# Moving one value load behind a key load, and the last head's mixer steps and their sum to earlier pairs

## The chip, the cores and the metric

The kernel runs on one core of one Trainium2 chip. The metric is the device time of the whole program in microseconds (us), as the median of several runs. The profile used below is one further execution of the same program, recorded by the hardware profiler.

## What is computed

A decode step of attention over a large cache, with a token-mixing MLP beside it, both added to the input:

```python
B, Sq, D = 8, 1, 512
Hq, Hkv, Sk, Dh = 32, 8, 8192, 128          # 4 query heads per key/value head
xn = layernorm(x)
q  = (xn @ wq) as (B, Hq, 1, Dh)
scores = q . k_cache * Dh**-0.5              # k_cache, v_cache: (8, 8, 8192, 128) float32
o  = softmax(scores) . v_cache
A  = o @ wo
h  = layernorm(xn)                           # the mixer: F = 1792 hidden units over one token
u  = gelu(h[b, d] * w1[f] + b1[f])           # (B, D, F)
Bo = sum_f u * w2[f] + b2
out = x + A + Bo
```

Nearly all bytes are the two caches: 64 pairs (8 key/value heads by 8 batch rows), each with 4 MiB of keys and 4 MiB of values, some 537 MB; `wq` and `wo` add 8 MiB each.

## The kernel before

The unit of work is a pair (h, b), key/value head h and batch row b, both counted from 0. The pairs run in order, b fastest. Everything is float32. There are two buffers of 4 MiB for keys, `K[b % 2]`, and two for values, `V[b % 2]`; at the start the two value buffers hold the two halves of `wq` until the queries have been projected from them (L193).

All large loads are issued by SyncE (SP) into one queue. An issue waits until its buffer is free, and every later issue stands behind it. The order of instructions on every engine is the order of the code; no scheduler moves them.

The function `slot(h, b)` is the work around one pair:

- `q_place` writes the query weights `w` of the next pair (DVE, L214).
- `qk(b)` forms the scores `s` of this pair from turned keys (PE, L228, 16 matmuls, shown as 32 records). When it has ended, its key buffer is free, and SP issues the load of the keys two pairs on.
- `turn(b + 1, ...)` transposes the next pair's keys in place, in four quarters (DVE, L222, about 2.3 us each). The first one waits until these keys have landed.
- `sm_max` (DVE, L234), `sm_bias` (PE, L238, then DVE, L239 and L240) and `sm_exp` (ACT, L243) are the softmax; `sm_place` (PE, L247, and DVE, L248) lays the result out as `pt`.
- `pv(b - 1)` multiplies the pair before by its values (PE, L255, again 16 matmuls, into `o`). When it has ended, its value buffer is free, and SP issues the value load of pair b + 1.
- `o_pick` (DVE, L260 to L263) and `o_place` (PE, L266) collect the output of pair b - 1.
- For each head the mixer takes 14 steps. `mx_step(j)` is one gelu on ACT (L312), a product on POOL (L313) and, but for j = 0, an addition to `macc` on POOL (L315). Both work on one buffer `g`, so a step waits for the one before. `mx_end` (PE, L319) sums `macc` over its partitions after the last step, and `y_add(mixed)` (DVE, L297) adds this to the output.

Exp and gelu need different tables on ACT: each change from one to the other is an ACT_TABLE_LOAD in front of the instruction.

In heads 0 to 6 a pair takes two mixer steps, and the sum is formed in the next head's first pair. The last head has no next head, so its steps are closer: steps 0 and 1 in pair 1, and then three each in pairs 2 to 5 (steps 2 to 4, 5 to 7, 8 to 10, 11 to 13). Its `mx_end` stands behind `qk(6)`. The pairs 6 and 7 of the last head are written out by hand after the loops (L408 to L443). There the keys of pair 7 come in four pieces, its values in pieces of a half, a quarter and two eighths, and the last part of `wo`, called `wo_end`, is loaded into the key buffer that has become free. At the end stand `o_last` (L269 to L272), `o_scale` (L285), `o_project` (L293), `y_add(proj)` (L297) and the store of the output (L443).

At the start, SP's queue is: `wq` in two halves, keys of pair (0, 0) in four pieces, keys of (0, 1), values of (0, 0), values of (0, 1), then from the slots keys of (0, 2), keys of (0, 3), values of (0, 2) and so on.

Of the kernel before, what the change touches and what calls it, by code (L numbers as in the profile page):

```python
# [24 lines left out]
NF = F // P  # L25
# [7 lines left out]
def attn_mixer_kernel(ctx: ExitStack, tc: tile.TileContext, x, kc, vc, wq, wo, w1, b1, w2, b2, out):  # L33
# [22 lines left out]
    V = [ring.tile([P, NT, DH], F32, name=f"v{k}") for k in range(2)]  # L56
# [8 lines left out]
    def load(to, src, h, b, pieces=(NT,)):  # L65
        rows = src[b, h, :, :].rearrange("(p t) d -> p t d", p=P)
        at = 0
        for n in pieces:
            nc.sync.dma_start(to[b % 2][:, at:at + n, :], rows[:, at:at + n, :])
            at += n  # L70
# [4 lines left out]
    def load_wo(h):  # L75
        nc.sync.dma_start(wo_t, wo.rearrange("(h r p) n -> h p r n", p=P, r=REP)[h])
# [136 lines left out]
    def q_place(h, b):  # L213
        nc.vector.tensor_tensor(W[b % 2].rearrange("p j (x r) -> p j x r", r=REP),  # L214
                                QT[:, h, b].unsqueeze(2).to_broadcast([P, NB, 2 * NB, REP]),
                                imask.rearrange("p i k -> p (i k)").unsqueeze(1).unsqueeze(3).to_broadcast([P, NB, 2 * NB, REP]), ALU.mult)
# [3 lines left out]
    def turn(b, a, w=NT // 4):  # L220
        t = K[b % 2][:, a:a + w, :].rearrange("p t d -> p (t d)")
        nc.vector.transpose(t, t)  # L222

    def qk(b):
        kt = K[b % 2].rearrange("p (u g) d -> p g u d", g=NG)
        for j in range(NB):
            for g in range(NG):
                nc.tensor.matmul(S[b % 2][g * Q:(g + 1) * Q, :], W[b % 2][:, j, :], kt[:, g, :, j * Q:(j + 1) * Q],  # L228
                                 start=(j == 0), stop=(j == NB - 1))
# [3 lines left out]
    def sm_max(b):  # L233
        nc.vector.tensor_reduce(MR, S[b % 2], AX.X, ALU.max)  # L234

    def sm_bias():
        m = misc()
        nc.tensor.matmul(m[:, :P], MR.to_broadcast([P, P]), nident, start=True, stop=True)  # L238
        nc.vector.tensor_tensor(SQ, m[:, :P], hmask, ALU.add)  # L239
        nc.vector.tensor_reduce(NBIAS, SQ, AX.X, ALU.min)  # L240

    def sm_exp(b):
        nc.scalar.activation(PR[b % 2], S[b % 2], AF.Exp, bias=NBIAS, scale=SCALE, accum_out=LR[:, b:b + 1])  # L243

    def sm_place(b):
        m = misc()
        nc.tensor.matmul(m, perm, PR[b % 2], start=True, stop=True)  # L247
        nc.vector.transpose(PT[b % 2], m)  # L248
# [3 lines left out]
    def pv(b, u0=0, u1=NU):  # L252
        for u in range(u0, u1):
            c = u % NB
            nc.tensor.matmul(O[b % 2][c * Q:(c + 1) * Q, :], PT[b % 2][:, u * Q:(u + 1) * Q],  # L255
                             V[b % 2][:, u * NG:(u + 1) * NG, :].rearrange("p t d -> p (t d)"),
                             start=(u < NB), stop=(u >= NU - NB))

    def o_pick(b):
        nc.vector.tensor_tensor(OM.rearrange("p (g d) -> p g d", g=NG), O[b % 2].rearrange("p (g d) -> p g d", g=NG),  # L260
                                dm.unsqueeze(2).to_broadcast([P, NG, DH]), ALU.mult)
        nc.vector.tensor_add(OB, OM[:, :256], OM[:, 256:])  # L262
        nc.vector.tensor_add(OB[:, :DH], OB[:, :DH], OB[:, DH:])  # L263

    def o_place(b):
        nc.tensor.matmul(MH[:, b * REP:(b + 1) * REP], OB[:, :DH], sel, start=True, stop=True)  # L266
# [10 lines left out]
    def o_sums():  # L277
        for r in range(REP):
            nc.tensor.matmul(sums[:, r * B:(r + 1) * B], sel[:, r:r + 1].to_broadcast([P, P]), LR, start=True, stop=True)

    def o_recip():
        nc.vector.reciprocal(RD, sums.rearrange("p (r b) -> p r b", r=REP))

    def o_scale():
        nc.vector.tensor_tensor(OTS.rearrange("p r (b s) -> p r b s", s=BS)[:, :, :, 0],  # L285
                                MH[:, :REP * B].rearrange("p (b r) -> p r b", r=REP), RD, ALU.mult)
# [3 lines left out]
    def o_project(w):  # L290
        for r in range(REP):
            for j in range(NB):
                nc.tensor.matmul(proj[j * Q:(j + 1) * Q, :], OTS[:, r, :], w[:, r, quarter[j]],  # L293
                                 start=(r == 0), stop=(r == REP - 1))

    def y_add(m):
        nc.vector.tensor_add(yacc, m, yacc)  # L297
# [3 lines left out]
    def mx_pick(h):  # L301
        nc.vector.tensor_tensor(BM, ident[:B, bass.ds(h, 1)], ident[:B, bass.ds(h, 1)], ALU.mult)
        nc.vector.tensor_tensor(BW, bsel[:, h, :], bsel[:, h, :], ALU.mult)

    def mx_begin():
        nc.tensor.matmul(MI[2], BM.to_broadcast([B, P]), hn, start=True, stop=True)

    def mx_copy():
        nc.scalar.copy(HB, MI[2])

    def mx_step(j):
        nc.scalar.activation(G, HB, AF.Gelu_apprx_tanh, bias=b1t[:, j:j + 1], scale=w1t[:, j:j + 1])  # L312
        nc.gpsimd.tensor_tensor(G if j else ACC, G, w2t[:, j:j + 1].to_broadcast([P, D]), ALU.mult)  # L313
        if j:
            nc.gpsimd.tensor_add(ACC, ACC, G)  # L315

    def mx_end():
        for j in range(NB):
            nc.tensor.matmul(mixed[j * Q:(j + 1) * Q, :], BW, ACC[:, quarter[j]], start=True, stop=True)  # L319
# [18 lines left out]

    q_project(first_turns)
    load(V, vc, 0, 0)  # L340
    load(V, vc, 0, 1)
    q_place(0, 0)


# [1 line left out]
    def after(h, b, n):  # L346
        return (h, b + n) if b + n < B else (h + 1, b + n - B)

    def slot(h, b, last=False, first=False):

        q_place(*after(h, b, 1))
        qk(b)
        load(K, kc, *after(h, b, 2), (NT // 4,) * 4 if last and b == B - 3 else (NT,))
        if b == 0 and not first:
            o_sums()
            mx_end()
        if b == 1:
            if not first:
                o_project(wo_t)
            mx_begin()  # L360
        turn(b + 1, 0)
        sm_max(b)
        if b == 0 and not first:
            o_recip()
        turn(b + 1, quart)
        if b or not first:
            pv(b - 1)
            load(V, vc, *after(h, b, 1))
        turn(b + 1, 2 * quart)
        sm_bias()  # L370
        if b or not first:
            o_pick(b - 1)
            o_place((b - 1) % B)
        if b < 2 and not first:
            y_add(proj if b else mixed)
        if first and b:
            mx_copy()
            mx_step(0)
            mx_step(1)
        sm_exp(b)  # L380
        turn(b + 1, 3 * quart)
        sm_place(b)
        if b == 0:
            if not first:
                o_scale()
            mx_pick(h)
        if b == 1 and not first:
            mx_copy()
        for j in range(3 * b - 4, 3 * b - 1) if last else range(2 * b - 2, 2 * b) if b and not first else ():
            mx_step(j)  # L390
        if b == 3 and not last:
            load_wo(h)

    tc.prologue_barrier()
    slot(0, 0, first=True)
    slot(0, 1, first=True)
    with tc.For_i(0, HKV - 1, 1, iteration_sync="staggered", head_align_engines=[nc.tensor.engine]) as h:
        for b in range(2, B + 2):
            slot(*after(h, b, 0))
            if b % 2 == 0:  # L400
                for e in (nc.tensor, nc.vector, nc.scalar, nc.gpsimd):
                    tc.previous_stage_wait(e.engine)
            elif b < B + 1:
                tc.stage_boundary()
    h = HKV - 1
# [2 lines left out]
    L = B - 1  # L408
    q_place(h, L)
    qk(L - 1)  # L410
    mx_end()
    turn(L, 0)
    turn(L, quart)
    sm_max(L - 1)
# [57 lines left out]
```

## Time and profile before

| | us |
|---|---|
| median of 3 runs | 1301.13 (1301.08 to 1301.55) |
| the profiled execution, whole | 1302.48 |
| its span | 1298.7 |
| DVE busy | 809.2 (62%) |
| PE busy | 780.6 (60%) |
| ACT busy | 289.8 (22%) |
| POOL busy | 251.8 (19%) |
| main DMA queue | 99.1% of 16 engines' span, 553.67 MB |

The span is what the trace covers; the whole time has 3.78 us more around it. Several engines are busy for more than half of the span, but only the DMA queue is busy nearly throughout. An average over the span hides a short stretch at either end, so the rows of single stretches have to be read: windows of 2 us, the timeline of an engine, and the chain of work that ended last, which gives at each step what released it.

### The profile page before, as it was taken

Reading aid. Unit: us, or ns where it says so; the run is one execution under the profiler, and the core shown is the slowest. Engines: PE = TensorE matmul, PEld = TensorE weight load, DVE = VectorE, ACT = ScalarE, POOL = GpSimd, SP = SyncE. Lnnn points to the kernel's source line nnn. Section 1 sums busy time; section 2 is a strip of 40 time slices with the busy share of each in tenths; the row PEclk is TensorE's granted clock in tenths of the full one; section 3 lists DMA queues with packets and bytes.
Section 4 is the critical chain, followed back from the end, with each engine's and each line's share of the span. In section 5 each row is a group of like instructions: output and inputs, shape, how many; then the busy total and the mean of one; then the engine's idle time right before and its main releaser. Section 6 shows DMA issues by size and latency. Waiting matters only on the chain.

```text
span 1298.7 us, 13708 instructions
## 1 busy us (share of the span) xinstructions
PE 780.6 (60%) x5178; PEld 250.2 (19%) x5178; DVE 809.2 (62%) x860; ACT 289.8 (22%) x366; POOL 251.8 (19%) x226
## 2 busy tenths in 40 slices
PE   3646457546566556666476565575565664666657
PEld 2212112112122111211122111121111221121112
DVE  3566665665765756755656747656557656567673
ACT  0103211212202213113221222113132132122230
POOL 0012221122112122022121122212221121211430
PEclk9768688777787786787776786777877877777878
DMA  9989999999999999999999999999999999999996
GB/s 403 434 377 435 431 434 432 430 426 441 435 435 428 430 436 435 435 428 431 435 436 434 429 430 435 436 434 430 430 434 436 434 433 428 433 436 434 431 427 268
DMA packets 24451, 553.93 MB, mean 427 GB/s; under 512 B 2508, under 2 KB 2540, under 8 KB 6900
## 3 DMA queue, kind: packets, MB, share of 16 engines
q1 hardware_dynamic: 24292, 553.67, 99.1%
q8 instruction: 12, 0.20, 0.1%
q0 software_dynamic: 128, 0.02, 0.0%
q10 hardware_dynamic: 16, 0.02, 0.0%
q14 instruction: 3, 0.02, 0.0%
HBM read 553.69 MB, written 0.02 MB: 426 GB/s over the span
## 4 chain that ended last, share of the span: by engine, by line
DMA 52%; DVE 21%; PE 18%; ACT 4%; issue 1%; POOL 1%; SPq 0%; ACTq 0%; DVEq 0%
DMA k<-in_A_k_cache_dram 52%; DVE k L222 17%; PE s L228 12%; PE misc L247 4%; ACT L243 2%; ACT pr L243 1%; DVE mr L234 1%; PE o L255 1%; DVE nb L240 1%; DVE sq L239 0%; PE mh L266 0%; DVE om L260 0%; POOL macc L315 0%; POOL g L313 0%; DVE ob L262 0%
## 5 line engine op out<-in xcount | busy, mean ns | idle before, releaser
L222 DVE STREAM_TRANSPOSE k<-k 128x2048 f32<-128x2048 f32 x256 | 582.0, 2292 | 396.2 <-DMA k<-in_A_k_cache_dram 396.1
L228 PE MATMUL s<-k,w 128*32 128x512 f32 x2048 | 318.4, 774 | 11.5 <-DVE k L222 8.4
L313 POOL TENSOR_TENSOR g<-g,w2t 128x512 f32<-128x512 f32 x104 | 108.1, 1039 | 718.9 <-ACT g L312 703.1
L266 PE MATMUL mh<-sel,ob 128*128 128x4 f32 x126 | 36.4, 359 | 346.8 <-DVE ob L263 346.8
L255 PE MATMUL o<-v,pt 128*32 128x512 f32 x2048 | 234.8, 598 | 0.8 <-DVE pt L248 0.8
L243 ACT ACT_TABLE_LOAD x56 | 71.8, 1283 | 683.5 <-DVE nb L240 683.5
L247 PE MATMUL misc<-pr,perm 128*128 128x512 f32 x128 | 129.9, 1117 | 15.5 <-ACT pr L243 12.6
L315 POOL TENSOR_TENSOR macc<-macc,g 128x512 f32<-128x512 f32 x104 | 132.4, 1273 | 9.6
L228 PEld LDWEIGHTS s<-k,w 128*32 128x32 f32 x2048 | 73.2, 139 | 293.3 <-issue 235.9
L312 ACT ACTIVATE g<-hb,b1t,w1t 128x512 f32<-128x512 f32 x112 | 91.1, 813 | 136.4 <-POOL macc L315 126.5
L238 PE MATMUL misc<-nident,mr 128*128 128x128 f32 x128 | 34.0, 350 | 110.7 <-DVE mr L234 110.7
L266 PEld LDWEIGHTS mh<-sel,ob 128*128 128x128 f32 x126 | 30.8, 304 | 360.8 <-DVE ob L263 360.0
L255 PEld LDWEIGHTS o<-v,pt 128*32 128x32 f32 x2048 | 62.3, 111 | 155.4 <-issue 153.6
L243 ACT ACTIVATE pr<-s,nb 128x512 f32<-128x512 f32 x64 | 44.0, 687 | 130.3 <-DVE nb L240 129.7
L248 DVE STREAM_TRANSPOSE pt<-misc 128x512 f32<-128x512 f32 x64 | 45.2, 707 | 42.0 <-PE misc L247 42.0
L312 ACT ACT_TABLE_LOAD x54 | 69.3, 1283 | 1.4
L313 POOL TENSOR_TENSOR macc<-g,w2t 128x512 f32<-128x512 f32 x8 | 8.3, 1039 | 286.9 <-ACT g L312 286.9
L238 PEld LDWEIGHTS misc<-nident,mr 128*128 128x128 f32 x128 | 20.8, 204 | 166.6 <-DVE mr L234 160.4
L234 DVE TENSOR_REDUCE mr<-s 128x1 f32<-128x512 f32 x64 | 41.8, 653 | 4.8 <-PE s L228 4.8
L260 DVE TENSOR_TENSOR om<-o,dm 128x512 f32<-128x512 f32 x63 | 42.9, 681 | 0.3 <-issue 0.3
L247 PEld LDWEIGHTS misc<-pr,perm 128*128 128x128 f32 x128 | 31.8, 307 | 22.2 <-ACT pr L243 20.2
L214 DVE TENSOR_TENSOR w<-qt,imask 128x128 f32<-128x128 f32 x64 | 29.8, 466 | 0.2 <-DVE pt L248 0.2
(77 smaller groups left out, 204.6 us busy)
## 6 DMA issues: line engine op xcount, KB each, us to landing
v<-in_A_v_cache_dram SPq DMA_DIRECT2D x63, 4096.0 KB, 27.5
k<-in_A_k_cache_dram SPq DMA_DIRECT2D x62, 4096.0 KB, 21.3
v<-in_A_wq_dram SPq DMA_DIRECT2D x2, 4096.0 KB, 12.7
k<-in_A_k_cache_dram SPq DMA_DIRECT2D x8, 1024.0 KB, 24.5
wo<-in_A_wo_dram SPq DMA_DIRECT2D x7, 1024.0 KB, 29.5
v<-in_A_v_cache_dram SPq DMA_DIRECT2D x1, 2048.0 KB, 7.7
v<-in_A_v_cache_dram SPq DMA_DIRECT2D x1, 1024.0 KB, 9.3
v<-in_A_v_cache_dram SPq DMA_DIRECT2D x2, 512.0 KB, 10.1
```

The costliest lines, as they stand in the source:

```text
L222: nc.vector.transpose(t, t)
L228: nc.tensor.matmul(S[b % 2][g * Q:(g + 1) * Q, :], W[b % 2][:, j, :], kt[:, g, :, j * Q:(j + 1) * Q], start=(j == 0), stop=(j == NB - 1))
L234: nc.vector.tensor_reduce(MR, S[b % 2], AX.X, ALU.max)
L238: nc.tensor.matmul(m[:, :P], MR.to_broadcast([P, P]), nident, start=True, stop=True)
L243: nc.scalar.activation(PR[b % 2], S[b % 2], AF.Exp, bias=NBIAS, scale=SCALE, accum_out=LR[:, b:b + 1])
L247: nc.tensor.matmul(m, perm, PR[b % 2], start=True, stop=True)
L248: nc.vector.transpose(PT[b % 2], m)
L255: nc.tensor.matmul(O[b % 2][c * Q:(c + 1) * Q, :], PT[b % 2][:, u * Q:(u + 1) * Q], V[b % 2][:, u * NG:(u + 1) * NG, :].rearrange("p t d - ...
L266: nc.tensor.matmul(MH[:, b * REP:(b + 1) * REP], OB[:, :DH], sel, start=True, stop=True)
L312: nc.scalar.activation(G, HB, AF.Gelu_apprx_tanh, bias=b1t[:, j:j + 1], scale=w1t[:, j:j + 1])
L313: nc.gpsimd.tensor_tensor(G if j else ACC, G, w2t[:, j:j + 1].to_broadcast([P, D]), ALU.mult)
L315: nc.gpsimd.tensor_add(ACC, ACC, G)
```

## The change

Two edits, which do not touch each other.

The load of the second values, pair (0, 1), no longer stands ahead of the slots. It is issued in slot (0, 0), by the same line that issues the value load in all other slots, and so behind the keys of pair (0, 2).

In the last head, the 12 mixer steps from 2 to 13 stand four each in pairs 2, 3 and 4, and none in pair 5. `mx_end` moves from behind `qk(6)` to the end of pair 5's slot, and so ahead of `qk(6)`.

```diff
     q_project(first_turns)
     load(V, vc, 0, 0)
-    load(V, vc, 0, 1)
     q_place(0, 0)
...
         if b or not first:
             pv(b - 1)
-            load(V, vc, *after(h, b, 1))
+        load(V, vc, *after(h, b, 1))
...
-        for j in range(3 * b - 4, 3 * b - 1) if last else range(2 * b - 2, 2 * b) if b and not first else ():
+        for j in range(4 * b - 6, min(4 * b - 2, NF)) if last else range(2 * b - 2, 2 * b) if b and not first else ():
             mx_step(j)
...
+        if b == 5 and last:
+            mx_end()
...
     qk(L - 1)
-    mx_end()
     turn(L, 0)
```

On SP, at the start of the program, with `v_86` and `v_87` the two value buffers and `k_84` and `k_85` the two key buffers. Before:

```order
L69 DMA k_84<-in_A_k_cache_dram 128x2048 x4
L69 DMA k_85<-in_A_k_cache_dram 128x8192
L69 DMA v_86<-in_A_v_cache_dram 128x8192
L69 DMA v_87<-in_A_v_cache_dram 128x8192
L69 DMA k_84<-in_A_k_cache_dram 128x8192
L69 DMA k_85<-in_A_k_cache_dram 128x8192
```

And now:

```order
L69 DMA k_84<-in_A_k_cache_dram 128x2048 x4
L69 DMA k_85<-in_A_k_cache_dram 128x8192
L69 DMA v_86<-in_A_v_cache_dram 128x8192
L69 DMA k_84<-in_A_k_cache_dram 128x8192
L69 DMA v_87<-in_A_v_cache_dram 128x8192
L69 DMA k_85<-in_A_k_cache_dram 128x8192
```

The keys of pair (0, 2), into `k_84`, have changed places with the values of pair (0, 1), into `v_87`; all that comes after them is as it was.

On PE, in the last head: the end of pair 5's slot (`o_place`, `sm_place`), then `qk(6)` (L228), `sm_bias(6)` (L238) and `pv(5)` (L255), as one piece of the difference:

```order
 L266 MATMUL mh<-sel,ob 128x4
 L247 MATMUL misc_174<-pr_157,perm 128x512
+L319 MATMUL mh<-macc,bw 32x128 x4
 L228 MATMUL s_169<-k_84,w_152 32x512 x16
-L319 MATMUL mh<-macc,bw 32x128 x4
 L238 MATMUL misc_175<-nident,mr 128x128
 L255 MATMUL o_172<-v_87,pt_155 32x512 x16
```

The four matmuls of the mixer's sum have moved from behind `qk(6)` to in front of it.

On ACT, in the last head, from the gelus of pair 4 to the exps of pairs 5 (`pr_157`), 6 (`pr_156`) and 7 (`pr_157`), as one piece of the difference:

```order
 L312 ACT_TABLE_LOAD
-L312 ACTIVATE g<-hb,b1t,w1t 128x512 x3
+L312 ACTIVATE g<-hb,b1t,w1t 128x512 x4
 L243 ACT_TABLE_LOAD
 L243 ACTIVATE pr_157,lr<-s_170,nb 128x512
-L312 ACT_TABLE_LOAD
-L312 ACTIVATE g<-hb,b1t,w1t 128x512 x3
-L243 ACT_TABLE_LOAD
 L243 ACTIVATE pr_156,lr<-s_169,nb 128x512
 L243 ACTIVATE pr_157,lr<-s_170,nb 128x512
```

Pair 4 has one gelu more, as pairs 2 and 3 have; pair 5's three gelus are gone, and with them the table load ahead of them and the one ahead of pair 6's exp.

## The prediction

> **What bounds the kernel now.** I read the page first: its line of GB/s, and the shares of the chain that ended last.
>
> ```profile
> GB/s 403 434 377 435 431 434 432 430 426 441 435 435 428 430 436 435 435 428 431 435 436 434 429 430 435 436 434 430 430 434 436 434 433 428 433 436 434 431 427 268
> DMA 52%; DVE 21%; PE 18%; ACT 4%; issue 1%; POOL 1%; SPq 0%; ACTq 0%; DVEq 0%
> ```
>
> Each of the 40 slices is 32.5 us. From the fourth to the last but one they hold 426 to 441 GB/s, so the queue carries all that it can there, and work between can be moved about without effect. Three slices fall short: the first, the third (377) and the last. The change touches the last two of these places. I then cut the third slice finer, by windows (us, busy time of each engine, granted clock of PE, DMA share, GB/s):
>
> ```profile
> 88.00:90.00 2.00, 2.00 (x12) 0.39 (x8) 0.61 (x1) 0.00 (x0) 0.00 (x0) 0.50 0.70 295
> 90.00:92.00 2.00, 2.00 (x20) 0.56 (x16) 0.07 (x1) 0.00 (x0) 0.00 (x0) 0.90 0.15 66
> 64.00:120.00 56.00, 31.58 (x194) 9.53 (x190) 36.85 (x36) 13.99 (x18) 10.44 (x10) 0.76 0.95 406
> 200.00:1200.00 1000.00, 610.06 (x3911) 190.29 (x3904) 636.35 (x652) 226.17 (x284) 193.08 (x168) 0.76 1.00 433
> ```
>
> The queue runs dry at 90 us. Against 433 GB/s, the 56 us at 406 have lost 56 x (1 - 406/433) = 3.5 us. What was late is in SP's own timeline (start, us, line, operation):
>
> ```profile
> 35.27 0.81 SPq L69 DMA_DIRECT2D v<-in_A_v_cache_dram  x2
> 43.45 18.34 SPq L69 DMA_DIRECT2D k<-in_A_k_cache_dram  x2
> 66.07 0.33 SPq L69 DMA_DIRECT2D v<-in_A_v_cache_dram  x1
> 92.10 0.35 SPq L69 DMA_DIRECT2D k<-in_A_k_cache_dram  x1
> ```
>
> In the chain, a DMA's length runs from issue to landing:
>
> ```profile
> 43.45 29.42 DMA k<-in_A_k_cache_dram
> 92.10 12.17 DMA k<-in_A_k_cache_dram
> 120.95 26.57 DMA k<-in_A_k_cache_dram
> 164.83 21.33 DMA k<-in_A_k_cache_dram
> 242.90 20.68 DMA k<-in_A_k_cache_dram
> 280.81 24.17 DMA k<-in_A_k_cache_dram
> ```
>
> And on DVE the first turn of keys (0,1), which had waited for them:
>
> ```profile
> 43.91 2.31 DVE L222 STREAM_TRANSPOSE k<-k 128x2048 f32<-128x2048 f32 x1 [4.02 <-DMA k<-in_A_k_cache_dram]
> ```
>
> The two value loads, pairs (0,0) and (0,1), are issued together at 35.27. Keys (0,1) land at 43.91. Keys (0,2), issued at 43.45, land at 43.45 + 29.42 = 72.87, three loads later (values 0, values 1, keys 2): 28.96/3 = 9.65 us a load. In the loop, landings at 120.95 + 26.57 = 147.52 and 164.83 + 21.33 = 186.16 lie four loads apart: 38.64/4 = 9.66. Where a load of `wo` lies between (263.58 to 304.98) the step is 41.40, so 1 MiB of `wo` takes 2.75. On this grid keys (0,3) end at 82.5 and values (0,2), issued at 66.07, at 92.2. Keys (0,4) are issued at 92.10: nothing is queued ahead of them. They wait for `qk(2)`, which waits for keys (0,2), which stood behind values (0,1), which nobody needed yet.
>
> Now the tail, by the timeline (start, us, engine and line; in brackets the idle time before and its releaser):
>
> ```profile
> 1259.23 4.57 PE L228 MATMUL s<-k,w 128*32 128x512 f32 x32
> 1264.91 0.65 DVE L234 TENSOR_REDUCE mr<-s 128x1 f32<-128x512 f32 x1
> 1267.13 1.26 POOL L315 TENSOR_TENSOR macc<-macc,g 128x512 f32<-128x512 f32 x1
> 1268.44 0.65 PE L319 MATMUL mh<-macc,bw 128*32 128x128 f32 x8 [4.64 <-POOL macc L315]
> 1269.03 0.80 PE L238 MATMUL misc<-nident,mr 128*128 128x128 f32 x2
> 1269.75 6.13 PE L255 MATMUL o<-v,pt 128*32 128x512 f32 x32
> 1270.62 1.28 ACT L243 ACT_TABLE_LOAD   x1 [4.69 <-DVE nb L240]
> 1270.66 4.50 DVE L222 STREAM_TRANSPOSE k<-k 128x2048 f32<-128x2048 f32 x2
> 1276.87 3.64 PE L228 MATMUL s<-k,w 128*32 128x512 f32 x32
> 1281.74 3.64 PE L255 MATMUL o<-v,pt 128*32 128x512 f32 x32
> 1290.31 1.92 PE L255 MATMUL o<-v,pt 128*32 128x512 f32 x16
> 1294.15 1.08 PE L293 MATMUL mh<-k,ots 128*32 128x128 f32 x32 [0.31 <-DVE ots L285]
> ```
>
> And two windows of it (PE's clock is the last but two):
>
> ```profile
> 1266.00:1268.00 2.00, 0.00 (x0) 0.00 (x0) 0.00 (x0) 0.00 (x0) 1.91 (x2) 1.00 1.14 492
> 1270.00:1272.00 2.00, 2.00 (x12) 0.40 (x8) 1.90 (x4) 1.37 (x2) 0.00 (x0) 0.50 1.06 459
> ```
>
> PE has ended `qk(6)` at 1263.80 and then stands 4.64 us in front of the mixer's sum, whose last POOL step ends at 1268.39. Behind it in PE's order waits `sm_bias(6)`, whose input is there at 1265.5; behind that on DVE the last two turns, and `qk(7)` at 1276.87 behind these and behind `pv(5)`. The idle time also costs clock: 1.00 before, 0.50 after, so `pv(5)` takes 6.13 where `pv(6)` takes 3.64. From `qk(7)` on PE hardly waits until the projection at 1294.15. So the tail is bound by PE and its wait for POOL, not by the queue.
>
> **The change part by part.** *The load.* Its issue (under 0.4 us on SP) moves past one issue, keys (0,2), which waits until 43.45 for `qk(0)`. Behind `qk(0)` the queue still holds values (0,0), to 43.91 + 9.66 = 53.6, so nothing runs dry; POOL's queue is not passed. Keys (0,2) then land at 63.2 and values (0,1) at 72.9, before `pv(1)` in the next slot wants them (keys (0,3) at 82.5 come first). All of slot 1 behind its first turn comes 9.66 earlier, keys (0,4) are issued near 82.4 with 10 us still queued, and the dry stretch is gone. Its price has three readings. Keys (0,4) landed at 104.27 where the grid has 72.87 + 3 x 9.66 = 101.85: 2.4. The bytes say 3.5. And keys (0,6) landed at 147.52, seven loads and one `wo` behind 72.87, where the grid has 72.87 + 67.6 + 2.75 = 143.2: 4.3. The first is taken when 16 engines start together on an empty queue and none lags, the last between two landings with a full queue. I take the bytes, which lie between: **3.5**, with 2.4 and 4.3 as ends. Since the queue is the bound up to the tail, all of it should arrive there.
>
> *The steps.* A fourth step is added to pairs 2, 3 and 4:
>
> ```profile
> 1226.41 0.81 ACT L312 ACTIVATE g<-hb,b1t,w1t 128x512 f32<-128x512 f32 x1 [2.51 <-POOL macc L315]
> 1235.70 1.28 ACT L243 ACT_TABLE_LOAD   x1 [8.48 <-DVE nb L240]
> 1247.72 1.28 POOL L315 TENSOR_TENSOR macc<-macc,g 128x512 f32<-128x512 f32 x1
> ```
>
> A step takes 0.81 + 2.50 = 3.31 us. The third gelu of pair 3 ends at 1227.22, a fourth at 1230.5, and the next exp's table load starts at 1235.70: 5 us of cover, so 0. In pair 4 the last addition now ends at 1249.00 + 3.31 = 1252.3. If this cover went, each further us would delay exp, `sm_place` and the next `qk`, though in pairs 2 to 4 still before the queue's bound.
>
> *The sum.* It reaches PE at 1259.2, 6.9 us after that addition, waits for nothing, and takes 0.65. It delays `qk(6)` to 1264.45, while `sm_max(6)` stands behind two turns until 1264.91: hidden, by 0.46. Without that cover its excess would be paid in full.
>
> *What then comes earlier.* `sm_bias(6)` starts at 1265.5 instead of 1269.03, that is 3.53 earlier, and takes 0.49 to 0.80. DVE's last turns end at 1270.66 + 4.50 - 3.53 = 1271.6. PE idles only 1.1 us; it had none to do from 1263.80 to 1268.44, and the window up to 1268 still shows 1.00, so the clock should hold, and `pv(5)` runs from 1266.1 to 1269.7. Exp(6) needs no table load (its 1.28 is gone, but lies beside `pv(5)`), and `sm_place(6)` ends at about 1270.9. `qk(7)` waits for the turns: 1271.6 instead of 1276.87, **5.3** earlier. Behind it the same instructions follow at the same clock, if the queue keeps up:
>
> ```profile
> 1249.07 27.68 SPq L69 DMA_DIRECT2D v<-in_A_v_cache_dram  x5
> 1276.84 0.96 SPq L81 DMA_DIRECT2D k<-in_A_wo_dram  x2
> ```
>
> The same transfers by size, with the us from issue to landing:
>
> ```profile
> v<-in_A_v_cache_dram SPq DMA_DIRECT2D x1, 4096.0 KB, 27.2
> v<-in_A_v_cache_dram SPq DMA_DIRECT2D x2, 512.0 KB, 10.1
> k<-in_A_wo_dram SPq DMA_DIRECT2D x1, 256.0 KB, 12.1
> ```
>
> Values 6 land at 1249.07 + 27.2 = 1276.3; `pv(6)` wants them at 1281.74 - 5.3 = 1276.4. Values 7 are now issued from about 1268 to 1270, well before the queue is empty, so by the grid they end at 1286.0 (`pv(7)`'s last part wants them at about 1286.5), and `wo_end` at 1288.7 (`o_project` wants it at 1294.15 - 5.3 = 1288.85). These fit with 0.1 to 0.5 to spare. If the last landing came no earlier than now, at the second issue of `wo`, about 1277.3, plus 12.1 = 1289.4, 4.75 would be left. So the tail gives 4.75 to 5.3; I take **5.2**, since its loads no longer wait for `pv(5)`.
>
> The sum: 3.5 + 5.2 = 8.7 off a span of 1298.7, so 1290.0, and 1293.8 for the profiled execution with its 3.78 around. That execution took 1302.48, 1.35 more than the median of the runs, so the median should go from 1301.13 to **1292.4**.
>
> **The rivals.** *The head gives little.* If the lag from 104.27 to 147.52 is not owed to the dry queue, the head gives 2.0 to 2.4, and the time is 1301.1 - 2.2 - 5.2 = 1293.7. For it: the landing at 104.27 is a direct measurement; against it: the bytes. Here the Trainium skill bears on the head: "DMA: Bandwidth & Descriptors", section "Anatomy of one DMA", gives each DMA a fixed cost of about 2.0 us, which a queue that never empties hides (it states this for another kind of queue than SP's). By it the head would give 2.0, an estimate from that page, and the time would be 1293.9; the row of 12.17 against 9.66 has 2.5.
>
> *The tail's clock stays at half.* If the clock drops in spite of the shorter gap, `pv(5)` takes 6.13 and `sm_place(6)` 2 us, so `qk(7)` starts at 1274.3: the tail gives 2.6 and the time is 1295.0. For it: `pv(5)` ran so now. Against it: the clock held for over 4 us of idle PE. The Trainium skill's "TensorE: Matmul & The Clock Gate", part on the HAM clock gate, has the clock fall after an idle window of about 3.4 us; a gap of 1.1 us is below that too.
>
> *The load changes nothing.* Were the third slice's loss due to something else, only the tail's 5.2 would stay: 1295.9. The issue at 92.10 with the queue empty speaks against it.
>
> *Slower: the sum stalls PE ahead of `qk(6)`.* Now only the softmax of pair 6 waits behind the sum; then `qk(6)` and all behind it would. It decides once the four steps of pair 4 end later than 1259.2, at 3.31 + 6.9/4 = 5.0 us a step. To end 0.2% (2.6 us) above now it must also eat the 8.7: 18.2 us over four steps, 7.9 us a step, for 1305 or so. The gelu at 1226.41 had waited 2.51 for POOL while DVE and PE were busy beside it, so a step of 7.9 us is remote.
>
> **How the numbers follow.** 0.2%, 2.6 us, is about what a measurement of this kernel can tell from no change. Forecast 0.62; little from the head 0.2; half clock in the tail 0.08; no gain from the load 0.04; less than 2.6 us either way, by several of these, 0.03; slower 0.03. The likeliest lies between 3.5 + 5.2 = 8.7 and its ends: 4.3 + 5.3 = 9.6 (1291.5) and 2.4 + 4.75 = 7.15 (1294.0). The range goes on to the half-clock case, 1295.0, and a little below the ends, since I have no row for the queue's last microseconds at full rate: 1290.8 to 1295.2. It leaves out some 0.12 (the last three cases, and a little of the first). Faster 0.94, same 0.03, slower 0.03.
>
> **What would show it.** Right: no window near 90 us below 250 GB/s, a third slice of 430 or more, keys (0,2) landing near 63, keys (0,4) issued near 82 and landing 20 us later; on PE, the sum without a wait in front of it, `pv(5)` near 3.6 us, some 5 us less from `qk(6)`'s end to `qk(7)`'s start. Wrong: a new dip later in the first 150 us, PE waiting for value pieces or `wo_end` by more than 1 us near the end, or a clock of 0.50 during `pv(5)`.

## The result, and the profile after

The changed kernel takes 1294.2 us (median of 5 runs, 1293.86 to 1294.46) where the kernel before, in the same series, takes 1301.55 (1301.08 to 1301.82): 7.35 us less, a ratio of 0.9944 with a 95% interval of 0.993 to 0.9959. The forecast was 1292.4 with a range of 1290.8 to 1295.2. Its profiled execution took 1293.86, where the forecast had 1293.8 for it, with a span of 1290.5.

The page's line of GB/s no longer has a dip in its third slice, and the queue's share has gone from 99.1% to 99.7%:

```profile
GB/s 405 428 433 430 431 436 436 428 436 431 432 437 431 433 435 429 436 436 428 437 431 433 437 427 436 435 430 436 432 431 437 432 432 435 429 436 434 429 427 331
q1 hardware_dynamic: 24292, 553.67, 99.7%
```

The windows of the head (busy times, PE's clock, DMA share, GB/s) now carry 430 GB/s over the 56 us that had 406, and the nearly empty window at 90 us (66 GB/s before) is gone:

```profile
88.00:90.00 2.00, 0.00 (x0) 0.00 (x0) 1.90 (x3) 0.00 (x0) 0.00 (x0) 0.93 0.87 377
90.00:92.00 2.00, 0.39 (x2) 0.39 (x2) 1.87 (x5) 1.80 (x2) 0.00 (x0) 0.50 0.99 426
64.00:120.00 56.00, 33.95 (x206) 9.91 (x202) 36.21 (x36) 13.41 (x17) 12.63 (x11) 0.76 1.00 430
```

The chain of waits, where a DMA's length runs from issue to landing, shows why: keys (0,2) land at 43.09 + 19.82 = 62.91, and keys (0,4) are issued at 81.68 instead of 92.10, with some 20 us from issue to landing instead of 12.17. The third row is keys (0,6), which land at 143.40 instead of 147.52:

```profile
43.09 19.82 DMA k<-in_A_k_cache_dram
81.68 19.88 DMA k<-in_A_k_cache_dram
119.47 23.93 DMA k<-in_A_k_cache_dram
```

In the tail, PE's timeline has the sum (L319) without a wait, `sm_bias(6)` at 1261.88, `pv(5)` at full clock (3.64 instead of 6.13) and `qk(7)` at 1267.75. New is the bracket of `pv(6)`, in the fifth row: it waits for a DMA.

```profile
1255.84 0.65 PE L319 MATMUL mh<-macc,bw 128*32 128x128 f32 x8
1261.88 0.49 PE L238 MATMUL misc<-nident,mr 128*128 128x128 f32 x2 [1.59 <-DVE mr L234]
1262.30 3.64 PE L255 MATMUL o<-v,pt 128*32 128x512 f32 x32
1267.75 3.64 PE L228 MATMUL s<-k,w 128*32 128x512 f32 x32 [0.76 <-DVE k L222]
1273.35 3.64 PE L255 MATMUL o<-v,pt 128*32 128x512 f32 x32 [0.66 <-DMA v<-in_A_v_cache_dram]
1281.92 2.11 PE L255 MATMUL o<-v,pt 128*32 128x512 f32 x16
1285.92 1.08 PE L293 MATMUL mh<-k,ots 128*32 128x128 f32 x32 [0.31 <-DVE ots L285]
```

### The profile page after: what moved, and what is told of

It reads as the page before. It is cut to its first block, busy times and chain, and to the rows that moved or that the text cites. A ratio compares the mean times of both kernels' runs of the same rounds, so it can differ in the third digit from the quotient of the medians.

```text
span 1290.5 us, 13705 instructions
## 1 busy us (share of the span) xinstructions
PE 778.6 (60%) x5178; PEld 249.8 (19%) x5178; DVE 809.2 (63%) x860; ACT 287.5 (22%) x364; POOL 252.1 (20%) x226
## 3 DMA queue, kind: packets, MB, share of 16 engines
q1 hardware_dynamic: 24292, 553.67, 99.7%
## 4 chain that ended last, share of the span: by engine, by line
DMA 53%; DVE 20%; PE 18%; ACT 3%; issue 2%; SPq 0%; DVEq 0%; ACTq 0%
DMA k<-in_A_k_cache_dram 51%; DVE k L222 16%; PE s L228 12%; PE misc L247 4%; DMA v<-in_A_v_cache_dram 2%; ACT L243 2%; ACT pr L243 1%; DVE mr L234 1%; PE o L255 1%; DVE nb L240 1%; DVE sq L239 0%; PE mh L266 0%; DVE om L260 0%; DVE ob L262 0%; DVE yacc L297 0%
## 5 line engine op out<-in xcount | busy, mean ns | idle before, releaser
L228 PE MATMUL s<-k,w 128*32 128x512 f32 x2048 | 319.0, 776 | 11.3 <-DVE k L222 9.2
L255 PE MATMUL o<-v,pt 128*32 128x512 f32 x2048 | 232.4, 593 | 1.5 <-DVE pt L248 0.8
L228 PEld LDWEIGHTS s<-k,w 128*32 128x32 f32 x2048 | 73.4, 139 | 292.4 <-issue 235.0
L238 PE MATMUL misc<-nident,mr 128*128 128x128 f32 x128 | 32.7, 339 | 101.8 <-DVE mr L234 101.6
L255 PEld LDWEIGHTS o<-v,pt 128*32 128x32 f32 x2048 | 62.1, 110 | 154.2 <-issue 151.5
L248 DVE STREAM_TRANSPOSE pt<-misc 128x512 f32<-128x512 f32 x64 | 45.3, 707 | 41.6 <-PE misc L247 41.6
L238 PEld LDWEIGHTS misc<-nident,mr 128*128 128x128 f32 x128 | 20.0, 196 | 158.5 <-DVE mr L234 155.1
```

## Experiments

Two quantities are read from every trace. The *head's shift* is how much earlier the keys of pair (0,6) land than at 147.52 in the first trace. The *tail's length* is the time from the first turn of the keys of pair (7,6), which waits for their landing, to the projection (L293): 1247.16 to 1294.15 = 47.0 us before, 1243.77 to 1285.92 = 42.15 after. Since the queue is full between the two, a gain in the one should add to a gain in the other.

**The load alone.**

```diff
-    load(V, vc, 0, 1)
...
-            load(V, vc, *after(h, b, 1))
+        load(V, vc, *after(h, b, 1))
```

> Only the load is moved; steps and sum as in the kernel before. Additive theory: keys (0,4) are issued near 82 and the dry stretch at 90 us goes; every key landing from pair (0,6) on comes 3.6 to 4.1 us earlier, and that shift is kept to the end, so about 1297.7. Rival, no part of the last head's loss of 0.8 us belongs to the steps: then this kernel also loses 0.8 us of its shift at the keys of pair (7,4), as the changed kernel did, and ends near 1298.3.

1297.73 us (9 runs, 1297.56 to 1299.24) against 1301.16 of the kernel before (15 runs, 1299.94 to 1302.70): 3.4 us less, ratio 0.9973 (0.9963 to 0.9983). The keys of pair (0,6) come 4.35 us earlier. The tail's length is 1244.08 to 1291.07 = 47.0, as before. So the load acts on the head only, and by the medians its price is close to what was forecast. The shift is not kept to the end, though: it falls from 4.4 to 3.1 us over the last head's pairs 3 to 6, without any change to the steps. Of the two theories put down, the first one's time came out, 1297.7, but the second one's loss of 0.8 us or more was there in the trace. The profiled run, 1299.24, is one of the two slowest of the nine, 1.5 us above the median, so the record does not say whether the seven faster runs lost it too.

**The tail alone.**

```diff
-        for j in range(3 * b - 4, 3 * b - 1) if last else range(2 * b - 2, 2 * b) if b and not first else ():
+        for j in range(4 * b - 6, min(4 * b - 2, NF)) if last else range(2 * b - 2, 2 * b) if b and not first else ():
...
+        if b == 5 and last:
+            mx_end()
...
-    mx_end()
```

> Only the steps and the sum are moved; the load as in the kernel before. Additive theory: no shift up to the last head, the sum without a wait, qk(7) 5.7 us earlier, and 4.1 to 4.9 us less at the projection: 1296.6 to 1297.4. If the fourth step in pair 2 is what costs the 0.8 us at the keys of pair (7,4), they land 0.8 us later than in the kernel before. Rival, the tail gains only because the queue is ahead from the start: less than 3 us.

1297.36 us (6 runs, 1296.07 to 1298.24) against the same 1301.16: 3.8 less, ratio 0.9968 (0.9956 to 0.998). The tail's length is 1246.66 to 1288.96 = 42.3, so 4.7 less. There is no loss at the keys of pair (7,4): the shift against the first trace is 0.5 us from pair (0,6) to the end. So the fourth step in pairs 2 to 4 costs nothing that this trace shows, and the loss comes only with the other edit. The two parts, 3.4 and 3.8, make 7.2 of the 7.35: they add, as far as intervals of more than 1 us to either side can tell.

**The steps alone, the sum in its old place.** The first two lines of that diff, without the others.

> Only the steps are closer, four each in pairs 2 to 4; the sum stays behind qk(6), the load as before. Theory: the wait for POOL goes because the steps have ended, so the sum runs at once in its old place, and the time is that of steps and sum together within 0.4 us. Rival, the place of the sum carries the gain: no more than 1 us faster than before.

1296.77 us (5 runs, 1296.44 to 1297.31), 4.4 less, ratio 0.9966 (0.9952 to 0.9979). PE's timeline has the sum behind `qk(6)` with no wait, and `sm_bias(6)` waiting for DVE as in the changed kernel:

```profile
1258.06 4.31 PE L228 MATMUL s<-k,w 128*32 128x512 f32 x32
1262.20 0.39 PE L319 MATMUL mh<-macc,bw 128*32 128x128 f32 x8
1264.10 0.49 PE L238 MATMUL misc<-nident,mr 128*128 128x128 f32 x2 [1.52 <-DVE mr L234]
```

The tail's length is 1245.99 to 1288.00 = 42.0. The medians of this and of steps and sum together are 0.6 apart, a little over the 0.4 expected, with intervals that overlap; the tails' lengths differ by 0.3. The steps carry the gain, and moving the sum adds nothing that shows.

**The sum alone, steps as before.** The last two pieces of that diff, without the first two lines: the forecast's slower rival.

> Only the sum is moved ahead of qk(6); three steps a pair up to pair 5, the load as before. This is the forecast's slower rival made to happen. Theory: PE stands in front of qk(6) from 1259.2 to 1268.4, qk(6) starts near 1269 at half clock, sm_bias(6) near 1274.2, the last turns end near 1280.4, and qk(7) starts 3.5 us later than before: about 1305. Rival, the place of the sum does not matter: within 0.5 us of before.

1305.91 us (6 runs, 1305.60 to 1306.75), 4.75 more than before, ratio 1.0037 (1.0024 to 1.0049).

```profile
1267.23 0.65 PE L319 MATMUL mh<-macc,bw 128*32 128x128 f32 x8 [9.13 <-POOL macc L315]
1267.65 6.18 PE L228 MATMUL s<-k,w 128*32 128x512 f32 x32
1274.66 0.49 PE L238 MATMUL misc<-nident,mr 128*128 128x128 f32 x2 [0.82 <-DVE mr L234]
1280.53 3.64 PE L228 MATMUL s<-k,w 128*32 128x512 f32 x32 [0.75 <-DVE k L222]
```

PE stands 9.13 us in front of the sum, and `qk(6)` behind it then runs at the low clock (0.50 in the windows from 1266 to 1272), 6.18 us instead of 4.57 before. The tail's length is 1245.96 to 1297.81 = 51.85, 4.9 more than before; I had expected 3.5. The mechanism is as described, and the same edit that is harmless behind four steps a pair costs nearly 5 us behind three.

**Half of values 6 left out.** On the changed kernel:

```diff
-        load(V, vc, *after(h, b, 1))
+        load(V, vc, *after(h, b, 1), (NT // 2,) if last and b == B - 3 else (NT,))
```

> The changed kernel, but the values of the last head's pair 6 are only half loaded (2 MiB left out; the other half of the buffer keeps old values). All later loads come 4.8 us earlier. Theory: the new tail is bound by the queue by less than 1 us, and right behind that by PE's own order from qk(7) on, so only PE's wait for values 6 (0.66) and for the last value pieces (0.15) goes: 0.8 us less than the changed kernel. Rival, the tail is bound by the queue alone: about 4.8 us less.

1293.62 us (4 runs, 1293.50 to 1294.12), with 1294.15 for the changed kernel on the same chip: 0.5 less, for 4.8 us less of transfer. The tail's length is 1244.0 to 1285.57 = 41.6, against 42.15, and no wait for a DMA is left on PE in it; `pv(6)` has no bracket any more:

```profile
1273.16 3.64 PE L255 MATMUL o<-v,pt 128*32 128x512 f32 x32
```

So the queue holds the new tail back by only some 0.5 us, and PE's own order comes right behind it.

**`sm_place(7)` inside `pv(6)`.** On the changed kernel:

```diff
-    pv(L - 1)
+    pv(L - 1, 0, 4)
     sm_place(L)
+    pv(L - 1, 4)
```

> The changed kernel, with pair 7's sm_place put behind the first 4 of the 16 matmuls of pv(6) instead of behind all of them, so that DVE's pt transpose (0.8 us in which PE waits) lies beside the other 12. Theory: PE reaches the last value pieces 0.75 us earlier, and then waits for them and for the last of wo, which lands some 0.4 us ahead of its use now: 0.3 to 0.5 us less. Rival, the queue is the bound already: no change.

1294.26 us (5 runs, 1294.15 to 1294.61) beside 1294.15: no change, and my expectation was wrong. PE's timeline shows the 0.8 us wait for `pt` gone and given back: the second half of `pv(7)` starts at 1281.49, but takes 2.77 us where the two traces of the changed kernel have 2.11 and 2.39, since the last value piece lands only at 1283.17.

```profile
1273.63 1.07 PE L255 MATMUL o<-v,pt 128*32 128x512 f32 x8 [0.69 <-DMA v<-in_A_v_cache_dram]
1274.63 1.13 PE L247 MATMUL misc<-pr,perm 128*128 128x512 f32 x2
1275.68 4.67 PE L255 MATMUL o<-v,pt 128*32 128x512 f32 x40
1281.49 2.77 PE L255 MATMUL o<-v,pt 128*32 128x512 f32 x16
```

Together with the half load this brackets the new bound: cutting PE's order alone gains nothing, and cutting the queue alone gains 0.5.

**The value load one place later still.** On the changed kernel, the values of pair (0,1) go behind the keys of pair (0,3):

```diff
+        if b == 1 and first:
+            load(V, vc, 0, 1)
...
-        load(V, vc, *after(h, b, 1))
+        if b or not first:
+            load(V, vc, *after(h, b, 1))
```

> The changed kernel, with the values of pair (0,1) put one place further back still, behind the keys of pair (0,3). Theory: what counts is that the queue never empties, and that is reached already, so the keys land earlier by 9.7 us in one pair and all is back on the same grid by the keys of pair (0,4): the same time within 0.4 us. Rival, earlier keys are worth something by themselves: 1 us or more faster.

1296.30 us (5 runs, 1295.77 to 1296.76), 2.15 more than the changed kernel's 1294.15. Neither expectation was right. The windows say why (the last two columns are DMA share and GB/s):

```profile
58.00:60.00 2.00, 2.00 (x24) 0.36 (x12) 0.00 (x0) 0.00 (x0) 0.00 (x0) 1.00 1.19 508
60.00:62.00 2.00, 2.00 (x14) 0.58 (x14) 0.00 (x0) 0.72 (x2) 0.00 (x0) 1.00 0.78 246
62.00:64.00 2.00, 2.00 (x24) 0.65 (x20) 1.10 (x1) 1.96 (x2) 0.00 (x0) 1.00 0.84 344
```

The chain has keys (0,2) landing at 42.44 + 20.44 = 62.88, and keys (0,6) at 120.95 + 23.74 = 144.69 instead of 143.1 to 143.4:

```profile
42.44 20.44 DMA k<-in_A_k_cache_dram
...
120.95 23.74 DMA k<-in_A_k_cache_dram
```

Keys (0,3) are issued at 60.24, 2.6 us before keys (0,2) land at 62.88, and in that window the rate falls to 246 GB/s all the same. A queue that is about to empty already costs. The theory that the queue must not empty stands; what was wrong is how much must still be in it.

The trace says why. It keeps the 16 reports that make up a landing, as many as there are DMA engines; the chain shows only the last of them. The reports for keys (0,2) run from 61.12 to 62.88, so at the issue the earliest engine had only 0.9 us of work left. Values (0,1), two loads later, have their earliest report at 81.66. That is 20.54 us behind, where two loads on a full queue take 19.32: 1.2 us were lost. In the kept traces this is most of the price: the projection starts 1.5 us later than in the changed kernel on the same chip (1287.71 against 1286.21). The kept run, 1295.77, is the fastest of its five.

**The changed kernel again.**

> The changed kernel once more, on the chip of these runs. It shows whether the loss of 0.8 us in the shift of the key landings, seen at pair (7,4) in its first trace and in the kernel with the load alone, comes again. If it belongs to the load's place: 0.8 us or more lost again near there, a shift of 4.1 to 4.4 before it, and a time 7 us under the kernel before. If it was chance: no loss in this trace.

1294.15 us (5 runs, 1294.01 to 1295.85) against 1300.81 (9 runs, 1300.48 to 1302.18): 6.7 less, ratio 0.9951 (0.9937 to 0.9964). The loss came again. In its DVE timeline the first turns of pairs (7,3) and (7,4) stand 20.43 us apart, in the kernel before 19.31:

```profile
1184.75 2.31 DVE L222 STREAM_TRANSPOSE k<-k 128x2048 f32<-128x2048 f32 x1 [6.23 <-DMA k<-in_A_k_cache_dram]
1205.18 2.31 DVE L222 STREAM_TRANSPOSE k<-k 128x2048 f32<-128x2048 f32 x1 [7.03 <-DMA k<-in_A_k_cache_dram]
```

```profile
1189.14 2.31 DVE L222 STREAM_TRANSPOSE k<-k 128x2048 f32<-128x2048 f32 x1 [6.22 <-DMA k<-in_A_k_cache_dram]
1208.45 2.31 DVE L222 STREAM_TRANSPOSE k<-k 128x2048 f32<-128x2048 f32 x1 [5.91 <-DMA k<-in_A_k_cache_dram]
```

## Why the prediction was right, and where its sizes were off

**The dry queue.** Right: the load moved as described, the dip at 90 us went, and the load alone is worth 3.4 us by the medians (2.2 to 4.8 by the interval) where the forecast took 3.5. Keys (0,6) land at 147.52 in the first trace; in the three other traces with the load in its old place they land near 147.0, 146.0 and 146.3, and in the five with it moved as in the change between 143.1 and 143.4. From mean to mean, 146.7 to 143.25, the shift is 3.45. The grid's 4.3 was too much because the first trace itself was late. The rival in which the head gives 2.0 to 2.4 does not fit the medians, though the interval of the load alone just reaches it. The 2.0, the estimate from the page "DMA: Bandwidth & Descriptors" of the Trainium skill, lies outside that interval.

The 16 reports show why three readings of one stretch differed. In the first trace those of values (0,2), ahead of the dry stretch, run from 90.08 to 92.18, and those of keys (0,4), behind it, from 103.78 to 104.27. On a full queue each would have come 9.66 later. So the earliest report lost 4.0 us, the last 2.4 and the mean 3.6: the landing alone, the reading of 2.4, saw the engine that lost least, and the bytes saw the mean. From the issue at 92.10 to the earliest report are 11.68 us, 2.0 more than 9.66, and in the three other traces with the load in its old place it is 2.0 more too. The fixed cost of about 2.0 us that the prediction took from that page of the Trainium skill, given there for another kind of queue, agrees with this. What comes on top is the time that an engine had stood empty before the issue. This is also part of how the first trace was late: keys (0,4) are issued at 92.10 there, and at 91.92, 91.12 and 91.00 in the other three.

**What the first trace hid.** Its execution was 0.93 above the later median of 1301.55, and the changed kernel's profiled one 0.34 below its own. Between these two executions alone the difference is 8.62, close to the forecast's 8.7, but in part by luck. 0.4 of it lies outside the spans, which the 8.7 had not counted. Inside them, the load gave 4.1 at keys (0,6) and lost 0.8 of it again in the last head, so that 3.4 arrived where 3.5 had been taken; the tail gave 4.8 where 5.2 had been taken. Against the medians' 7.35 the gain was forecast 1.35 too large: the sum was made on a trace that was itself late, and the offset of 1.35 to the median was carried over as if it would stay. Such scatter is common here: the kernel before has 1299.94 to 1302.70 in the 15 runs beside the first experiments, and the changed kernel 1294.01 to 1295.85 in its second series.

**The steps and the sum.** Right in mechanism: no wait in front of the sum, `sm_bias(6)` earlier, the clock kept, and the fourth step without effect on exp, whose table loads still wait for DVE. The half-clock rival fell: `pv(5)` took 3.64, and the clock stayed at 1.00 from 1258 to 1268 through idle gaps of 1.59 and 0.76. The rule that the prediction took from the Trainium skill's "TensorE: Matmul & The Clock Gate" (part on the HAM clock gate), that the clock falls after a longer idle window, agrees. The term was a little too large. `qk(7)` came 29.71 - 23.98 = 5.7 us earlier, counted from the first turn of pair (7,6), but the tail only 4.8. The step that failed is "These fit with 0.1 to 0.5 to spare": values 6 landed 27.92 us after their issue, not 27.2 (28.4 and 28.9 in two later traces), so `pv(6)` waited 0.66 and started only 5.0 earlier, and the wait for the last pieces took another 0.2. The forecast's lower end, 4.75, which kept the old landing of `wo_end`, was nearer than the 5.2 I took. The load left half out gives back 0.5.

**What was not foreseen.** With the load moved as in the change, the shift falls in the last head, by 0.8 to 1.3 us, in all five traces; with it in its old place, in none of the other three. With the load one place later still it falls too, by 1.6 us, but only at keys (7,6). The steps don't cause it (the load alone shows it, the steps alone don't), and the windows around it show no dip in GB/s.

The record points at a cause that no run has tested: the queue that the page calls `instruction`, with 12 packets in all, of 16 KB and some 0.9 us each.

```profile
q8 instruction: 12, 0.20, 0.1%
```

In none of the ten traces does one of them fall between 200 and 1170 us, and over that stretch the shift of each trace stays within 0.2 us. Four fall between 1170 and 1250, where it changes in the six traces with the load moved. In the changed kernel's second trace the 16 reports for keys (7,3) lie within 1.93 us; of those for keys (7,4) fifteen lie within 1.97, and the last comes 3.11 behind the first. So one engine of the 16 had fallen behind by 1.1 us, and the landing waits for the last one. This fits an instruction packet that falls to the engine that is last already; on another engine it would leave the landing where it is.

**The slower rival** was rightly remote for this change, and real where its condition holds: with three steps a pair the sum ahead of `qk(6)` makes the kernel 4.75 slower.

## What to carry to other kernels

When one queue bounds a kernel, look at its first loads in order: one that nobody needs yet, ahead of one whose landing lets the next be issued, can empty the queue later. Issue with several microseconds still queued: 2.6 us ahead of the last landing was not enough here, because the engine that ended first had 0.9 us left. A side computation in the last iterations is best ended early rather than placed late, since an engine that waits for it also delays, and may slow, what stands behind. And a sum made on one trace needs a look at how far such traces scatter at that very place.

## What the runs showed of the hardware

A queue that was 2.6 us from its last landing had already fallen to 246 GB/s of 433. The 16 reports of a 4 MiB load were spread over 1.8 us (61.12 to 62.88) on a full queue, and over 0.5 us (103.78 to 104.27) behind an empty one. From the issue into an empty queue to the earliest report it took 11.6 to 11.7 us in four traces, against 9.66 for a load on a full queue. The landing of the same keys behind an emptied queue differed by 1.5 us between executions (146.0 to 147.5), against 0.3 us where the queue had stayed full.
